# ELU in the last layer: the clamp to negative values leaves VectorE, and the final step becomes a maximum against the pre-activation

## The chip, the cores and the metric

The kernel runs on one core of one Trainium2 chip. The metric is the device time of one execution in microseconds. PE is TensorE (PEld its weight loads), ACT is ScalarE, DVE is VectorE, POOL is GpSimd, and SP issues most of the DMAs.

## The reference

Three layers follow one another: attention with pooled queries, a mixture of eight experts of which each token uses two, and a dense layer with an ELU. Only the last one is touched. Its input `x` has 1152 rows of 512 values, `w_in` is 512 x 2048 and `w_out` is 2048 x 512:

```python
def _moe2_ref(x, w_in, w_out):
    h = x @ w_in
    alpha = 1.0
    g = np.where(h > 0.0, h, alpha * (np.exp(np.minimum(h, 0.0)) - 1.0))
    return (g @ w_out).astype(np.float32)
```

## The kernel before, in words

The whole program is scheduled by hand: each helper files its steps on a time line (`Line.at(t, step)`), the steps are sorted by that time, and the sorted order is the program order on every engine. Each engine then works through its own queue in that order and waits on semaphores. The planned times set only the order.

Every matrix product is done in split precision. A float32 value is held as a high part (rounded, made by a copy on ACT) and a low part (value less high part, made by a subtraction on DVE or POOL), and three matmul passes, high x high, low x high and high x low, add up in PSUM.

The last layer works in three chunks of 384 rows (`ch` 0 to 2). In a chunk, the 2048 hidden columns are 16 steps `f` of 128 columns. Three functions in `plan_moe2` (line 959 on) belong to each step:

- `l1(f)`: 12 matmuls into a PSUM tile `a` of 128 x 384 (line 972). There are three such tiles, each in a bank of its own.
- `act(f)`: the ELU from `a` to `r`, and the split of `r` into `g2h` (ACT, line 981) and `g2l` (DVE, line 982). The tiles `r` and `m` have two buffers each, `g2h` and `g2l` three.
- `outs(f)`: nine matmuls into three PSUM tiles `o` that run over all 16 steps (line 991). Of each three the first two read `g2h`, and the third reads `g2l`.

On PE the order is l1(0), l1(1), l1(2), outs(0), l1(3), outs(1), and so on, since `outs(f)` is filed two steps behind `l1(f)`.

While chunk 0 runs, the second halves of `w_in` and `w_out` are still brought in, in eight pieces of 128 x 1024 (`plan_weight`, line 681). For each piece SP loads `raw` (line 668, six buffers), ACT copies it into the high part `wh` (line 670), and POOL subtracts to get the low part `wl` (line 674). On ACT these copies stand between the ELU steps, in the order act(0), piece 0, act(1), pieces 1 and 2, act(2), piece 3, act(3), piece 4, act(4), pieces 5 and 6, act(5), piece 7, act(6). From act(7) on ACT has no weight pieces. For chunks 1 and 2 the expert outputs are gathered by POOL (line 942), mixed on DVE (lines 947 and 948), transposed on PE (line 955) and split (lines 956 and 957), while the chunk before is still at work.

In the experts, line 733 is an operation on DVE with the same kinds of operands as the changed last step of the ELU: one input in PSUM, one in SBUF, the result in SBUF.

Of the kernel before, what the change touches and what calls it, by code (L numbers as in the profile page):

```python
# [5 lines left out]
AF=mybir.ActivationFunctionType; OP=mybir.AluOpType; AX=mybir.AxisListType  # L6
# [135 lines left out]
def ap(src, off, dims):  # L142
    return bass.AP(tensor=src.tensor, offset=src.offset+off, ap=dims)
# [819 lines left out]
def plan_moe2(ln, tc, ch, t0, xs_, win, wout, out, gp, xp, ps):  # L963
    nc=tc.nc; O={}; G={}
    def l1(f):
        xh,xl=xs_['x']
        a=G['a',f]=ps.tile([128,512],FT,tag="a",name="a2",bufs=3)
        wh,wl=win[f//8]['w']; fs=slice((f%8)*128,(f%8)*128+128)
        n=0
        for wv,xv in ((wh,xh),(wl,xh),(wh,xl)):  # L970
            for c in range(4):
                nc.tensor.matmul(a[:,0:384],wv[:,c,fs],xv[:,c],start=n==0,stop=n==11); n+=1  # L972
    def act(f):
        a=G.pop(('a',f))
        r=gp.tile([128,384],FT,name="r2"); m=gp.tile([128,384],FT,name="m2")
        nc.scalar.activation(r,a[:,0:384],AF.Relu)  # L976
        nc.vector.tensor_scalar(m,a[:,0:384],0.0,None,op0=OP.min)  # L977
        nc.scalar.activation(m,m,AF.Exp)  # L978
        nc.vector.scalar_tensor_tensor(r,m,-1.0,r,op0=OP.add,op1=OP.add)  # L979
        gh=gp.tile([128,384],FR,name="g2h",bufs=3); gl=gp.tile([128,384],FR,name="g2l",bufs=3)  # L980
        nc.scalar.activation(gh,r,AF.Copy)  # L981
        nc.vector.tensor_tensor(gl,r,gh.bitcast(FT),op=OP.subtract)
        G[f]=(gh,gl)
    def outs(f):
        if f==0:
            for i in range(3): O[i]=ps.tile([128,512],FT,tag="o",name="o2",bufs=3)
        wh,wl=wout[f//8]['w']; gh,gl=G.pop(f)
        for i in range(3):
            ts=slice(i*128,i*128+128)
            for n,(gv,wv) in enumerate(((gh,wh),(gh,wl),(gl,wh))):  # L990
                nc.tensor.matmul(O[i],gv[:,ts],wv[:,f%8],start=f==0 and n==0,stop=f==15 and n==2)  # L991
    def fin(i):
        tt=3*ch+i
        y=xp.tile([128,512],FT,name="yg0",bufs=3) if ch==2 else gp.tile([128,512],FT,name="out_sb",bufs=2)
        if i%2: nc.vector.tensor_copy(y,O[i])
        else: nc.scalar.activation(y,O[i],AF.Copy)
        if tt<8:
            b,j=divmod(tt,4)
            nc.sync.dma_start(ap(out,(b*576+j)*512,[[2048,128],[1,512]]),y)
        else:  # L1000
            for b,e in enumerate((nc.sync,nc.scalar)):
                e.dma_start(ap(out,(b*576+512)*512,[[512,64],[1,512]]),y[64*b:64*b+64])
    d=3.87
    for f in range(16):
        ln.at(t0+d*f+(.05 if f==0 else 0),l1,f); ln.at(t0+d*f+1.0,act,f); ln.at(t0+d*(f+2)+.1,outs,f)
    for i in range(3): ln.at(t0+d*17+.2+.01*i,fin,i)
# [132 lines left out]
```

## Time and profile before

| what | value |
|---|---|
| median of 3 runs | 825.7 us (825.38 to 841.67) |
| the profiled execution | 819.85 us |
| its span, first to last instruction | 818.1 us |
| PE busy | 786.0 us, 96% of the span |
| DVE busy | 585.6 us, 72% |
| ACT busy | 482.4 us, 59% |
| POOL busy | 328.2 us, 40% |

The span leaves out 1.75 us of the profiled execution, ahead of its first and behind its last instruction. The last layer's matmuls begin 606.3 us into the span. Busy shares are averages over the whole span; what a change in the last layer is worth is read from the stretch from there on.

### The profile page before, as it was taken

Reading aid. Unit: us, or ns where it says so; the run is one execution under the profiler, and the core shown is the slowest. Engines: PE = TensorE matmul, PEld = TensorE weight load, DVE = VectorE, ACT = ScalarE, POOL = GpSimd, SP = SyncE. Lnnn points to the kernel's source line nnn. Section 1 sums busy time; section 2 is a strip of 40 time slices with the busy share of each in tenths; the row PEclk is TensorE's granted clock in tenths of the full one; section 3 lists DMA queues with packets and bytes.
Section 4 is the critical chain, followed back from the end, with each engine's and each line's share of the span. In section 5 each row is a group of like instructions: output and inputs, shape, how many; then the busy total and the mean of one; then the engine's idle time right before and its main releaser. Section 6 shows DMA issues by size and latency. Waiting matters only on the chain.

```text
span 818.1 us, 13530 instructions
## 1 busy us (share of the span) xinstructions
PE 786.0 (96%) x4891; PEld 721.4 (88%) x4891; DVE 585.6 (72%) x1182; ACT 482.4 (59%) x1109; POOL 328.2 (40%) x303
## 2 busy tenths in 40 slices
PE   7999999999999999989999999999999899999997
PEld 5898989998888889979899999999887799999996
DVE  6888898898999876586968778687555644454443
ACT  5988888989888864434444445445345434334432
POOL 4634051431510765266666677666516602000000
PEclk8999999999999999989999999999999999999999
DMA  8029465131002245559688898986743203001001
GB/s 251 2 93 274 136 230 178 40 128 57 29 30 105 91 138 198 187 179 309 228 287 262 274 306 279 295 275 218 263 125 115 64 14 104 1 14 38 1 1 40
DMA packets 50984, 119.82 MB, mean 146 GB/s; under 512 B 7574, under 2 KB 8598, under 8 KB 50914
## 3 DMA queue, kind: packets, MB, share of 16 engines
q1 hardware_dynamic: 47922, 109.35, 40.6%
q0 software_dynamic: 2912, 9.44, 3.6%
q8 instruction: 40, 0.66, 0.3%
q14 instruction: 30, 0.25, 0.1%
q10 hardware_dynamic: 80, 0.13, 0.0%
HBM read 82.89 MB, written 36.01 MB: 145 GB/s over the span
## 4 chain that ended last, share of the span: by engine, by line
PE 30%; DMA 11%; DVE 9%; ACT 3%; issue 2%; POOL 2%; SPq 0%; DVEq 0%; POOLq 0%; ACTq 0%
PE o L991 11%; PE a L972 10%; PE oe L741 5%; DMA raw<-in_moe_w_in_dram 5%; DMA raw<-in_moe_w_dram 3%; PE ae L731 3%; DVE wl L674 2%; DMA raw<-in_moe_w_out_dram 2%; ACT wh L670 1%; DVE cvt L703 1%; DVE cvm L701 1%; DVE r L979 1%; DMA raw<-wf 1%; POOL cvm L708 1%; DVE cvt L704 1%
## 5 line engine op out<-in xcount | busy, mean ns | idle before, releaser
L293 ACT ACTIVATE p<-sp,m 128x384 f32<-128x384 f32 x216 | 125.1, 585 | 13.2 <-DVE m L285 13.0
L282 DVE TENSOR_REDUCE m<-sp 128x1 f32<-128x384 f32 x216 | 115.4, 550 | 20.6 <-PE sp L277 18.8
L674 POOL TENSOR_TENSOR wl<-raw,wh 128x1024 fp32r<-128x1024 f32 x32 | 80.8, 2530 | 59.3 <-ACT wh L670 59.2
L670 ACT ACTIVATE wh<-raw 128x1024 fp32r<-128x1024 f32 x76 | 79.8, 1057 | 37.9 <-DMA raw<-in_moe_w_dram 36.7
L305 DVE TENSOR_TENSOR pl<-t_p,ph 128x512 fp32r<-128x512 f32 x144 | 96.8, 683 | 6.0 <-ACT ph L302 4.2
L302 ACT ACTIVATE ph<-t_p 128x512 fp32r<-128x512 f32 x144 | 86.2, 603 | 16.7 <-PE t_p L299 11.3
L299 PE MATMUL t_p<-ident,p 128*128 128x128 f32 x576 | 83.3, 274 | 1.2 <-ACT xt L363 0.7
L277 PE MATMUL sp<-khl,qh 128*128 128x384 f32 x192 | 75.6, 394 | 4.2 <-ACT p L293 3.7
L299 PEld LDWEIGHTS t_p<-ident,p 128*128 128x128 f32 x576 | 67.9, 140 | 9.9 <-ACT xt L363 0.9
L707 POOL TENSOR_SCALAR cvm<-cvm 128x512 f32<-128x512 f32 x32 | 51.3, 1602 | 38.9 <-DVE cvm L701 38.9
L277 PE MATMUL sp<-khl,ql 128*128 128x384 f32 x192 | 65.7, 342 | 0.0
L674 DVE TENSOR_TENSOR wl<-raw,wh 128x1024 fp32r<-128x1024 f32 x44 | 63.4, 1453 | 2.6 <-ACT wh L670 2.6
L310 PE MATMUL o<-ph,vhl 128*128 128x512 f32 x144 | 63.8, 443 | 0.0
L991 PE MATMUL o<-wh,g2h 128*128 128x512 f32 x144 | 57.1, 396 | 3.9 <-ACT g2h L981 3.9
L234 POOL TENSOR_SCALAR kr<-kraw 128x576 fp32r<-128x576 f32 x14 | 9.5, 678 | 126.2 <-PE t_k L241 126.2
L311 PE MATMUL o<-pl,vhl 128*128 128x512 f32 x144 | 57.3, 398 | 1.0 <-DVE pl L305 1.0
L991 PE MATMUL o<-wh,g2l 128*128 128x512 f32 x144 | 56.8, 394 | 0.0
L991 PE MATMUL o<-wl,g2h 128*128 128x512 f32 x144 | 56.3, 391 | 0.0
L977 DVE TENSOR_SCALAR m<-a 128x384 f32<-128x384 f32 x48 | 26.7, 556 | 40.9 <-ACT r L976 40.2
L708 POOL TENSOR_TENSOR cvm<-cvm,cvt 128x512 f32<-128x512 f32 x32 | 48.0, 1501 | 17.3 <-DVE cvt L704 17.3
L979 DVE SCALAR_TENSOR_TENSOR r<-m,r 128x384 f32<-128x384 f32 x48 | 34.3, 714 | 28.4 <-ACT m L978 27.8
L701 DVE TENSOR_SCALAR cvm<-raw 128x512 int32<-128x512 int32 x32 | 26.9, 839 | 34.8 <-DMA raw<-in_moe_w_in_dram 19.9
(269 smaller groups left out, 1987.4 us busy)
## 6 DMA issues: line engine op xcount, KB each, us to landing
raw<-in_moe_w_dram SPq DMA_DIRECT2D x60, 512.0 KB, 7.1
raw<-in_moe_w_in_dram SPq DMA_DIRECT2D x16, 512.0 KB, 7.7
wf<-cvm SPq DMA_DIRECT2D x32, 256.0 KB, 2.8
raw<-in_moe_w_out_dram SPq DMA_DIRECT2D x16, 512.0 KB, 8.3
raw<-wf SPq DMA_DIRECT2D x16, 512.0 KB, 4.6
xs<-zrow SPq DMA_DIRECT2D x3, 1792.0 KB, 15.1
xs<-zrow SPq DMA_DIRECT2D x2, 2560.0 KB, 22.9
xe<-xs SPq DMA_DIRECT2D x7, 672.0 KB, 9.4
```

Of the source, the lines that this page charges most:

```text
L277: nc.tensor.matmul(sp[:,g,0:384],w,kh[:,h,384*(g0+g):384*(g0+g)+384],start=i==0,stop=i==len(ops)-1)
L282: nc.vector.tensor_reduce(m[:,x:x+1],s['s',j,x][:,:,0:384],axis=AX.XY,op=OP.max,negate=True)
L293: nc.scalar.activation(s['p',j][:,384*g0:384*(g0+nb)].rearrange("p (g n) -> p g n",g=nb),s.pop(('s',j,x))[:,:,0:384],AF.Exp,bias=m[:,3:4], ...
L299: nc.tensor.transpose(t[:,jj*128:jj*128+128],s['p',4*h+jj][:,kt*128:kt*128+128],ident)
L302: nc.scalar.activation(ph,s['tp',h,kt],AF.Copy)
L305: nc.vector.tensor_tensor(pl,s.pop(('tp',h,kt)),s['ph',h,kt].bitcast(FT),op=OP.subtract)
L310: nc.tensor.matmul(s['o',h],w,s.pop(('ph',h,kt)),start=kt==0,stop=False)
L311: nc.tensor.matmul(s['o',h],w,s.pop(('pl',h,kt)),start=False,stop=kt==8)
L670: s.tc.nc.scalar.activation(w[0][:,p['i']*p['n']:(p['i']+1)*p['n']],p['r'],AF.Copy)
L674: e.tensor_tensor(w[1][:,sl],p['r'],w[0][:,sl].bitcast(FT),op=OP.subtract)
L972: nc.tensor.matmul(a[:,0:384],wv[:,c,fs],xv[:,c],start=n==0,stop=n==11); n+=1
L991: nc.tensor.matmul(O[i],gv[:,ts],wv[:,f%8],start=f==0 and n==0,stop=f==15 and n==2)
```

## The change

The ELU took four instructions per step: Relu on ACT, a minimum with zero on DVE, Exp on ACT, and on DVE the sum of (exp less one) and the Relu. It now takes three: ACT computes Relu(-h), then Exp of the negative of that, and DVE takes the maximum of (exp less one) and h, which it reads from PSUM. The split that follows is as it was.

```diff
     def act(f):
         a=G.pop(('a',f))
         r=gp.tile([128,384],FT,name="r2"); m=gp.tile([128,384],FT,name="m2")
-        nc.scalar.activation(r,a[:,0:384],AF.Relu)
-        nc.vector.tensor_scalar(m,a[:,0:384],0.0,None,op0=OP.min)
-        nc.scalar.activation(m,m,AF.Exp)
-        nc.vector.scalar_tensor_tensor(r,m,-1.0,r,op0=OP.add,op1=OP.add)
+        nc.scalar.activation(m,a[:,0:384],AF.Relu,scale=-1.0)
+        nc.scalar.activation(m,m,AF.Exp,scale=-1.0)
+        nc.vector.scalar_tensor_tensor(r,m,-1.0,a[:,0:384],op0=OP.add,op1=OP.max)
         gh=gp.tile([128,384],FR,name="g2h",bufs=3); gl=gp.tile([128,384],FR,name="g2l",bufs=3)
         nc.scalar.activation(gh,r,AF.Copy)
         nc.vector.tensor_tensor(gl,r,gh.bitcast(FT),op=OP.subtract)
```

## Rows read from the trace of the kernel before

**Rows 1.** Chain that ended last, from the page: shares of the span by engine

```profile
PE 30%; DMA 11%; DVE 9%; ACT 3%; issue 2%; POOL 2%; SPq 0%; DVEq 0%; POOLq 0%; ACTq 0%
```

**Rows 2.** Stretches of the last layer: length, busy us (x instructions) per engine, PEclk, DMA

```profile
606.30:645.50 39.20, 35.27 (x174) 30.07 (x173) 21.56 (x26) 19.56 (x34) 21.80 (x11) 1.00 0.37 119
...
672.00:690.00 18.00, 18.00 (x99) 16.41 (x98) 7.26 (x14) 7.46 (x16) 4.92 (x5) 1.00 0.38 117
690.00:740.00 50.00, 50.00 (x257) 45.56 (x256) 25.19 (x46) 19.55 (x39) 0.94 (x1) 1.00 0.02 6
```

**Rows 3.** Timeline, PE, starts of l1(3), l1(10) and l1(12) in chunk 0

```profile
614.96 0.86 PE L972 MATMUL a<-x2h,wh 128*128 128x384 f32 x4
...
649.48 0.86 PE L972 MATMUL a<-x2h,wh 128*128 128x384 f32 x4
...
657.75 0.86 PE L972 MATMUL a<-x2h,wh 128*128 128x384 f32 x4
```

**Rows 4.** Single lines: the ELU's instructions, duration ns min/median/max, first and last start

```profile
L976 ACT ACTIVATE r<-a x48: 469/493/499, 609.1 to 807.5; 128x384 f32<-128x384 f32 x48
L977 DVE TENSOR_SCALAR m<-a x48: 548/558/559, 609.6 to 808.0; 128x384 f32<-128x384 f32 x48
L978 ACT ACTIVATE m<-m x48: 523/525/528, 610.2 to 808.6; 128x384 f32<-128x384 f32 x48
L979 DVE SCALAR_TENSOR_TENSOR r<-m,r x48: 557/558/2728, 610.7 to 809.2; 128x384 f32<-128x384 f32 x48
L981 ACT ACTIVATE g2h<-r x48: 522/525/527, 611.3 to 809.8; 128x384 fp32r<-128x384 f32 x48
L982 DVE TENSOR_TENSOR g2l<-r,g2h x48: 557/559/561, 611.9 to 810.3; 128x384 fp32r<-128x384 f32 x48
```

**Rows 5.** Timeline, pieces 1 and 2, act(2) and outs(2): start us, us, [idle before <-releaser]

```profile
616.16 1.99 ACT L670 ACTIVATE wh<-raw 128x1024 fp32r<-128x1024 f32 x2
...
617.29 4.74 POOL L674 TENSOR_TENSOR wl<-raw,wh 128x1024 fp32r<-128x1024 f32 x2 [2.00 <-ACT wh L670]
...
618.06 0.47 ACT L976 ACTIVATE r<-a 128x384 f32<-128x384 f32 x1
...
618.57 0.56 DVE L977 TENSOR_SCALAR m<-a 128x384 f32<-128x384 f32 x1 [1.72 <-ACT r L976]
...
619.16 0.53 ACT L978 ACTIVATE m<-m 128x384 f32<-128x384 f32 x1 [0.62 <-DVE m L977]
619.72 2.73 DVE L979 SCALAR_TENSOR_TENSOR r<-m,r 128x384 f32<-128x384 f32 x1 [0.59 <-ACT m L978]
...
622.48 0.52 ACT L981 ACTIVATE g2h<-r 128x384 fp32r<-128x384 f32 x1 [2.79 <-DVE r L979]
...
623.03 0.56 DVE L982 TENSOR_TENSOR g2l<-r,g2h 128x384 fp32r<-128x384 f32 x1 [0.59 <-ACT g2h L981]
623.05 0.50 PE L991 MATMUL o<-wh,g2h 128*128 128x512 f32 x1 [1.72 <-ACT g2h L981]
```

**Rows 6.** Waits in the last layer, 606 us on: us in total, times, longest

```profile
PEld o L991 <- ACT g2h L981: 5.1, 5, 2.5
PE o L991 <- ACT g2h L981: 3.9, 2, 2.2
```

**Rows 7.** Timeline in the experts: DVE beside a POOL subtraction

```profile
473.17 2.89 POOL L674 TENSOR_TENSOR wl<-raw,wh 128x1024 fp32r<-128x1024 f32 x1 [0.46 <-ACT wh L670]
474.37 0.51 DVE L733 SCALAR_TENSOR_TENSOR hl<-ae,hh 128x336 fp32r<-128x336 f32 x1 [0.57 <-ACT hh L732]
474.79 1.55 DVE L701 TENSOR_SCALAR cvm<-raw 128x512 int32<-128x512 int32 x1
```

**Rows 8.** Single lines: DVE with an input in PSUM, weight subtractions, duration ns min/median/max

```profile
L733 DVE SCALAR_TENSOR_TENSOR hl<-ae,hh x56: 493/501/510, 363.8 to 581.5; 128x336 fp32r<-128x336 f32 x56
...
L957 DVE TENSOR_TENSOR x2l<-t,x2h x8: 548/553/560, 673.3 to 744.0; 128x384 fp32r<-128x384 f32 x8
...
L674 POOL TENSOR_TENSOR wl<-raw,wh x32: 2365/2407/3340, 337.7 to 639.6; 128x1024 fp32r<-128x1024 f32 x32
```

**Rows 9.** Timeline, DVE: an instruction that reads what the one before it wrote

```profile
651.82 0.48 DVE L947 TENSOR_SCALAR yg<-yg,wt 128x512 f32<-128x512 f32 x1
652.33 0.75 DVE L948 SCALAR_TENSOR_TENSOR yg<-yg,wt,yg 128x512 f32<-128x512 f32 x1
```

**Rows 10.** Groups of ACT instructions: a function table load (mean ns)

```profile
L448 ACT ACT_TABLE_LOAD x2 | 2.6, 1283 | 0.0
```

**Rows 11.** Timeline, SP: loads of the eight pieces, with the time their issue took

```profile
604.16 15.91 SPq L668 DMA_DIRECT2D raw<-wf x8
```

## The prediction

> **What bounds the kernel now.** The chain of waits comes first: half of its attributed time is PE, and DVE and ACT together have 12% [rows 1]. That is the whole program; the change touches only the last layer, so the stretches of that layer come next. [...] The first stretch, 606.3 to 645.5, is different: PE is busy 35.27 of 39.20 us. So the gain must come from there, if from anywhere.
>
> How much is lost there is read best from the spacing of l1. Seven steps lie between l1(3) and l1(10): 649.48 - 614.96 = 34.52 us, where seven undisturbed ones take 7 x 4.135 = 28.94 us [rows 3]. PE loses 5.58 us. The waits say to whom: TensorE's matmuls and weight loads of outs wait for g2h [rows 6]. (The 3.9 us of idle PE are two long gaps; the other 1.7 us are matmuls stretched because their weights come late.)
>
> Why g2h is late is seen at act(2) [rows 5]. Two things add up. First, the ELU is a relay between two engines, with ACT held in its queue meanwhile: Relu at 618.06, the minimum at 618.57, although it reads nothing that the Relu writes (both read the same PSUM bank, and the second reader starts when the first has ended), Exp at 619.16. Second, the last DVE step, line 979, takes 2.73 us, where its median is 0.558 [rows 4, 5]. It starts 0.06 us after the second of POOL's two subtractions must have begun (617.29 + half of 4.74 = 619.66), and ends 0.42 us after POOL's end at 622.03. Both of its inputs lie in SBUF, as POOL's do. Over 48 instructions only six are long, at the six steps in which a piece of weights is being subtracted; line 982, also with two SBUF inputs, always comes after the stall and never exceeds 0.561 us [rows 4]. Meanwhile ACT waits 2.79 us for DVE, and the next weight copy and Relu are queued behind that wait on ACT.
>
> **The change part by part.** *The minimum goes.* 48 x 0.558 = 26.8 us of DVE time are removed [rows 4]. On the path of a step Relu start to Exp start was 619.16 - 618.06 = 1.10 us [rows 5]; it becomes the Relu, 0.49 us, and a handover from ACT to itself. The trace before has no ACT instruction that reads what the one before it on ACT wrote. The nearest row is DVE's pair, where the reader starts 0.03 us after the writer's end (651.82 + 0.48 = 652.30 to 652.33) [rows 9]; the far one is a table load of 1.28 us in between [rows 10]. I take 0.03, since both are in-order engines that hand over a tile; the lower bound is an overlapped start, some 0.1 us less. The path is shorter by 1.10 - 0.52 = 0.58 us per step.
>
> *The scale of -1* is an operand of ACT instructions that exist already. Nothing is added; I keep 0.493 and 0.525 us [rows 4].
>
> *The last DVE step reads PSUM in place of one SBUF tile.* Its undisturbed price: line 957, one input in PSUM and 384 columns, has 0.553 us, where line 982 with two SBUF inputs has 0.559 [rows 4, 8]. I take 0.558, so nothing. [...]
>
> Its disturbed price is the larger point. The same kind of instruction, line 733, starts at 474.37 in the middle of a POOL subtraction (473.17 to 476.06) and takes 0.51 us; none of its 56 exceeds 0.510, while the neighbour of 474.79, of another kind, stretches to 1.55 us, 0.28 us past POOL's end [rows 7, 8]. So I expect line 979's successor to pass POOL, and the excess of the six stalls, 0.77 to 2.17 us each (1.33 to 2.73 less 0.56), to leave the path from Relu to g2h.
>
> *The stall goes to g2l.* It still has two SBUF inputs and now arrives while POOL works. I let it end 0.42 us after POOL, as line 979 did [rows 5]. Behind it on DVE stands only the next step's maximum, and on PE the third of each three matmuls.
>
> *The tile `a` is held until the maximum ends*, 0.16 + 0.49 + 0.03 + 0.53 + 0.03 + 0.56 = 1.8 us after l1, and l1(f+3) comes three steps later, over 10 us. No cost.
>
> **The sum, step by step.** I lay out chunk 0 with these durations: Relu 0.49, Exp 0.53, maximum 0.56, g2h 0.53, handovers 0.03, a weight copy 1.05 (0.1 of it overlapped), POOL 2.41 [rows 4, 5, 8]. ACT's round of a step is 2.2 us plus its pieces. With PE undisturbed, outs(f) starts at 612.90 + 4.135 f (614.96 less the 2.06 of outs(0)). Then:
>
> - act(1): Relu 612.1, g2h done 614.3, g2l 615.1 (POOL's piece 0 ends 614.7). Needed 617.0.
> - act(2): pieces 1 and 2 copied 614.2 to 616.2, POOL on them 615.3 to 620.1; Relu 616.1, g2h 618.3, g2l 620.1 + 0.42 = 620.5. Needed 621.2. Before: g2h 623.0.
> - act(3): Relu 619.2, g2h 621.6, g2l 622.9. Needed 625.3.
> - act(5): pieces 5 and 6 copied 624.6 to 626.6, POOL until 630.5; g2h 628.7, g2l 630.9. Needed 633.6. Before: 638.6.
>
> All are in time, with at least 0.6 us to spare. All of the 5.58 us is regained. The weights don't stand in the way: six of the eight loads were issued ahead of the ELU, the last two wait for a `raw` buffer [rows 11], which piece 0 frees at 614.7 instead of 615.3. Later stretches stay as they are, since PE has no idle time to give back [rows 2], and everything shifts with it.
>
> Span: 818.1 - 5.6 = 812.5 us; profiled execution 819.85 - 5.6 = 814.3. The median of the runs before lies 5.9 us above the profiled execution. I put the same 5.6 us on it: **825.7 - 5.6 = 820.1 us**, 0.7% less.
>
> **The rivals.** *(A) The stalls stay half on the path.* Either the maximum still waits for POOL, or POOL's subtractions, delayed by DVE, take the 3.34 us that the longest had [rows 8]. With the first, act(2)'s g2l ends at 621.9 and act(5)'s at 635.5, so that outs(2) loses 0.4 and outs(5) 1.2 us: 1.6 of the 5.6 us remain, 821.7 us. With the second, POOL ends pieces 1 and 2 at 622.0 and g2l ends 622.4, some 0.8 us too late, and again at pieces 5 and 6: also 821.7. [...] The six stalls before show VectorE as the loser each time.
>
> *(B) Nothing is gained.* PE finds another late input: the weight pieces, or at the chunk borders the gathered rows. For: ACT and POOL are both busier in the first stretch than later. Against: act(7) on has no pieces, and between 672 and 690, at a chunk border, PE has no gap [rows 2]. 825.7 us.
>
> *(C) It is slower: Exp behind its own Relu waits on ACT.* If the handover costs x more than 0.03 us, every step's round on ACT grows by x. In the seven steps with weight pieces the margin is used up at x = 0.5 us; at 1.3, a table load's length, 3.1 us are lost and the gain is 2.5 (823.2); from about x = 1.65 on the kernel is slower than before. From 2.0 on the round, 2.2 + x, exceeds PE's 4.135 in all 48 steps, and near x = 2.3 the kernel is some 2% slower. Against: Relu, Exp and Copy already alternate on ACT and no table load stands in the last layer; all of ACT's waits there have other names.
>
> **How the numbers follow.** Forecast 0.77, (A) 0.10, (B) 0.08, (C) with a time above 825.7 0.05. The likeliest is 820.1. The range: downward the whole gain on the level of the profiled execution, 814.3; upward it takes in (A) and (B) with the runs' spread of 0.3 us, 826. Faster or slower by over 2% (about what a measurement of this kernel can tell from no change) means 16.5 us, three times what PE loses here: faster 0.01, slower 0.03, within 0.96.
>
> **What would show it.** Right: seven steps from l1(3) to l1(10) in 28.9 us; no PE wait for g2h; the maximum at 0.55 to 0.57 us in all 48; line 982's longest growing from 0.56 to about 2.2 us; Exp starting 0.5 us after Relu. Wrong: a maximum over 1 us (A); PE waiting for g2l (A) or a weight (B); a gap between Relu and Exp (C). The sum is wrong as a whole if the median and the profiled execution do not move together.

## The result, and the profile after

| | before | changed |
|---|---|---|
| median of 7 runs each | 825.7 us (815.79 to 841.67) | 809.97 us (808.61 to 822.57) |
| ratio | | 0.9849, 95% interval 0.9809 to 0.9889 |
| profiled execution, its span | 819.85 us, 818.1 us | 822.57 us, 820.8 us |
| mean granted clock in the profiled execution | 0.990 | 0.980 |

By the ratio the changed kernel is 1.5% faster, some 12.5 us; the medians of the table lie 15.7 us apart. The prediction said 5.6 us, and 809.97 lies below its range. The executions of either kernel differ in how long TensorE was granted only half its clock (0.50) ahead of the last layer: every ratio in this document leaves out the longest ones, which the medians and ranges include, and as the profiled execution of the changed kernel is one of these, the traces are compared by stretches of the last layer and not by their spans.

The same stretch as in [rows 2], counted from the first l1 of each kernel (length, then busy us and instructions of PE, PEld, DVE, ACT, POOL, then PEclk, DMA share and GB/s):

```profile
614.60:653.80 39.20, 39.15 (x203) 35.95 (x202) 19.49 (x25) 23.19 (x40) 25.05 (x13) 1.00 0.45 146
698.00:748.00 50.00, 50.00 (x259) 45.36 (x258) 18.15 (x33) 18.86 (x38) 0.95 (x1) 1.00 0.02 6
```

PE is busy in 39.15 of 39.20 us, where it had 35.27, and handles 203 matmuls instead of 174. Later stretches were full and are full (50.00 of 50.00 us in both). The starts of l1(3) and l1(10), as in [rows 3]:

```profile
623.31 0.86 PE L972 MATMUL a<-x2h,wh 128*128 128x384 f32 x4
...
652.24 0.86 PE L972 MATMUL a<-x2h,wh 128*128 128x384 f32 x4
```

That is 28.93 us for the seven steps, 5.59 less than the 34.52 of [rows 3]. It is 4.133 us a step, where an undisturbed one took (657.75 - 649.48) / 2 = 4.135 [rows 3]: no time is left between them. From the first l1 to the last outs the layer takes 201.6 us against 207.2. The single lines of the ELU, as in [rows 4] (duration ns min/median/max):

```profile
L976 ACT ACTIVATE m<-a x48: 469/492/502, 617.4 to 810.2; 128x384 f32<-128x384 f32 x48
L977 ACT ACTIVATE m<-m x48: 523/523/527, 617.9 to 810.7; 128x384 f32<-128x384 f32 x48
L978 DVE SCALAR_TENSOR_TENSOR r<-m,a x48: 541/555/555, 618.5 to 811.3; 128x384 f32<-128x384 f32 x48
L981 DVE TENSOR_TENSOR g2l<-r,g2h x48: 557/559/2358, 619.7 to 812.4; 128x384 fp32r<-128x384 f32 x48
```

The last step, now line 978, never exceeds 0.555 us; the longest was 2.728. The subtraction, now line 981, has taken the stalls over: 2.358 where the longest was 0.561. Act(2) in the timeline, as in [rows 5]:

```profile
623.67 17.87 POOL L674 TENSOR_TENSOR wl<-raw,wh 128x1024 fp32r<-128x1024 f32 x7 [0.62 <-ACT wh L670]
624.45 0.47 ACT L976 ACTIVATE m<-a 128x384 f32<-128x384 f32 x1
624.95 0.53 ACT L977 ACTIVATE m<-m 128x384 f32<-128x384 f32 x1
625.51 0.55 DVE L978 SCALAR_TENSOR_TENSOR r<-m,a 128x384 f32<-128x384 f32 x1 [2.04 <-ACT m L977]
626.10 0.53 ACT L980 ACTIVATE g2h<-r 128x384 fp32r<-128x384 f32 x1 [0.62 <-DVE r L978]
...
626.66 2.20 DVE L981 TENSOR_TENSOR g2l<-r,g2h 128x384 fp32r<-128x384 f32 x1 [0.59 <-ACT g2h L980]
```

Relu to Exp is 0.50 us instead of 1.10; the maximum runs while POOL subtracts and is not held; g2h follows at once; g2l is held and nothing on PE waits for it. Of the waits of PE on ACT and DVE in the ELU [rows 6] none is left. So the last layer did what the forecast says: 5.59 us where 5.58 were forecast. The rest, some 7 us by the ratio and 10 by the medians, is the question.

### The profile page after: what moved, and what is told of

Read it like the earlier page. It is cut to its first block, busy times and chain, and to the rows that moved or that the text cites. A ratio compares the mean times of both kernels' runs of the same rounds, so it can differ in the third digit from the quotient of the medians.

```text
span 820.8 us, 13443 instructions
## 1 busy us (share of the span) xinstructions
PE 790.5 (96%) x4891; PEld 728.2 (89%) x4891; DVE 559.7 (68%) x1134; ACT 483.1 (59%) x1109; POOL 328.1 (40%) x303
## 4 chain that ended last, share of the span: by engine, by line
PE 31%; DMA 11%; DVE 10%; issue 2%; POOL 2%; ACT 1%; SPq 0%; DVEq 0%; POOLq 0%; ACTq 0%
PE a L972 12%; PE o L990 12%; DMA raw<-in_moe_w_in_dram 4%; DMA raw<-in_moe_w_out_dram 4%; PE oe L741 3%; DVE wl L674 3%; PE ae L731 3%; DVE cvt L703 2%; DVE cvm L701 2%; DVE cvt L704 1%; DMA ys<-ye 1%; POOL cvm L708 1%; DVE hl L733 1%; PE ac L922 1%; DVE cvt L702 1%
## 5 line engine op out<-in xcount | busy, mean ns | idle before, releaser
L978 DVE SCALAR_TENSOR_TENSOR r<-m,a 128x384 f32<-128x384 f32 x48 | 26.6, 554 | 86.3 <-ACT m L977 86.2
L976 ACT ACTIVATE m<-a 128x384 f32<-128x384 f32 x48 | 23.4, 488 | 64.4 <-PE a L972 64.4
L981 DVE TENSOR_TENSOR g2l<-r,g2h 128x384 fp32r<-128x384 f32 x48 | 33.4, 695 | 28.4 <-ACT g2h L980 28.4
```

## The experiments

### Is the rest of the gain the change, or the clock?

First the changed kernel and the kernel before were run again, unaltered, in the same session.

> The changed kernel once more, timed beside the kernel before. Two theories for why the whole gained 12.5 us at the medians when the last layer should give 5.6. Theory 1 (the rest is the granted clock of the runs drawn, not the change): each run's time goes with its mean granted clock, about 8.2 us per 0.01 of clock missing; carried to a clock of 1.00 the changed kernel is at 806 us and the kernel before at 811.7, 5.6 apart, and the ratio of the medians moves towards 0.993 as runs are added. Theory 2 (the change itself gives some 6 us more, somewhere ahead of the last layer or in it): at equal clock the two stay 10 to 12 us apart, or the changed kernel's runs have the higher clock time after time and the ratio stays at 0.985. Either way the trace's last layer, from its first l1 matmul to its last outs matmul, takes 201.2 us against 207.2 before.

> The kernel before against itself. Theory 1: the ratio is 1.00, but its runs scatter over 10 us or more with the granted clock (0.98 to 0.995), so a comparison of medians can be off by several us. Theory 2: its runs lie within 3 us of one another and the ratio is 1.000 with a narrow interval.

| | runs | median | mean clock of the runs | ratio to before |
|---|---|---|---|---|
| before | 35 | 818.79 us | 0.959 to 0.998 | |
| the same, again | 12 | 823.89 us | 0.961 to 0.994 | 1.005, 1.0014 to 1.0086 |
| changed | 12 | 814.84 us | 0.960 to 0.997 | 0.9951, 0.9909 to 0.9993 |

The ratio of the changed kernel moved from 0.985 to 0.995. Six of the first seven runs of the changed kernel had a mean clock of 0.991 to 0.997; of these twelve only half had 0.99 or more. The kernel before differs from itself by 5 us at the median and by half a per cent in the ratio, with an interval that leaves out 1; that is nearly as much as the effect looked for (5.6 us, 0.7%). The time follows the clock closely. Over all 94 runs of the kernel before that list their clock and the 31 of the changed one, both with the later ones below, a straight line with one slope for both gives 7.5 us per 0.01 of clock (8.2 were expected), and at equal clock the changed kernel is 5.1 us faster (standard error 0.4). With the runs of 0.975 and more alone it is 5.4 us. Theory 1 holds: at equal clock 5 to 5.5 us, the rest was which runs were drawn. The layer itself takes 201.6 us in this trace too; the 201.2 in the expectation was 0.4 too low.

Where the clock is lost stands in the traces. This is the end of attention, first in the changed kernel's first trace, then in its second:

```profile
300.00:310.00 10.00, 9.04 (x62) 8.31 (x61) 6.80 (x34) 5.64 (x12) 0.68 (x3) 0.86 0.89 311
310.00:320.00 10.00, 10.00 (x57) 9.98 (x57) 4.34 (x25) 3.43 (x4) 1.23 (x2) 0.50 0.02 8
320.00:330.00 10.00, 10.00 (x49) 8.44 (x48) 2.82 (x6) 1.41 (x4) 8.43 (x15) 0.79 0.54 176
```

```profile
300.00:310.00 10.00, 9.03 (x76) 8.44 (x75) 6.88 (x40) 5.03 (x10) 0.68 (x3) 1.00 0.82 305
310.00:320.00 10.00, 10.00 (x78) 8.84 (x76) 6.02 (x20) 4.12 (x7) 6.28 (x9) 1.00 0.30 86
```

In the first PE runs at a granted clock of 0.50 for some 17 us, and does 57 matmuls from 310 to 320 us, for which the second, at 1.00, shows 78. What PE did before it is the same in both, with two short gaps. First the trace in which the clock fell, behind the second gap, then the one in which it stayed:

```profile
305.53 0.29 PE L367 MATMUL t_l<-wd,xt 128*64 128x16 f32 x2 [0.31 <-ACT xt L363]
306.43 0.34 PE L844 MATMUL a<-x0h,w0h 128*128 128x168 f32 x1 [0.61 <-DVE L L371]
```

```profile
304.09 0.29 PE L367 MATMUL t_l<-wd,xt 128*64 128x16 f32 x2 [0.31 <-ACT xt L363]
304.99 0.34 PE L844 MATMUL a<-x0h,w0h 128*128 128x168 f32 x1 [0.61 <-DVE L L371]
```

Both have 0.31 and 0.61 us of idle time in front of the same instructions. So have all eleven traces here of kernels whose gaps are as they were (0.60 in two), and the clock falls there in six of them, for some 17 us or more, and not in the other five. The first trace of the kernel before, on which the prediction rests, is one of the five. What decides whether it falls is not shown.

### Which part of the change gives the 5.6 us?

Two things were changed in the last layer: the relay ACT, DVE, ACT, DVE lost one hand-over, and the last step lost one of its two SBUF inputs. Three kernels take them apart. The first changes the last step alone (against the kernel before):

```diff
         nc.scalar.activation(r,a[:,0:384],AF.Relu)
         nc.vector.tensor_scalar(m,a[:,0:384],0.0,None,op0=OP.min)
         nc.scalar.activation(m,m,AF.Exp)
-        nc.vector.scalar_tensor_tensor(r,m,-1.0,r,op0=OP.add,op1=OP.add)
+        nc.vector.scalar_tensor_tensor(r,m,-1.0,a[:,0:384],op0=OP.add,op1=OP.max)
```

> Only the last line of the ELU is changed: the maximum of (exp less one) and the pre-activation in PSUM. The Relu on ScalarE and the minimum on VectorE stay, the Relu's result being overwritten unread. Theory 'port' (what cost PE its 5.6 us is the last VectorE step waiting for POOL, since both its inputs lay in SBUF): the last step is 0.55 us in all 48, the subtraction g2l takes the stalls, PE waits for nothing, the last layer takes 201.2 to 201.7 us like the changed kernel's. Theory 'relay' (the hand-overs ACT, DVE, ACT cost it): the Relu to Exp time stays 1.1 us and most of the loss stays, the last layer takes 204 us or more.

The second shortens the relay but keeps both inputs in SBUF (against the changed kernel):

```diff
         nc.scalar.activation(m,a[:,0:384],AF.Relu,scale=-1.0)
         nc.scalar.activation(m,m,AF.Exp,scale=-1.0)
-        nc.vector.scalar_tensor_tensor(r,m,-1.0,a[:,0:384],op0=OP.add,op1=OP.max)
+        nc.scalar.activation(r,a[:,0:384],AF.Relu)
+        nc.vector.scalar_tensor_tensor(r,m,-1.0,r,op0=OP.add,op1=OP.add)
```

> The other part alone: the minimum on VectorE goes, ScalarE makes Relu(-h), Exp and Relu(h), and the last VectorE step adds (exp less one) and the Relu, both in SBUF as before. Theory 'port': the last step is stretched again in six steps, and PE loses 1.2 to 5.5 us, how much depending on whether the step starts just before or just after POOL's second subtraction; the last layer takes 202.5 to 207 us. Theory 'relay': the loss goes, 201.2 to 201.7 us.

The third keeps the clamp on VectorE and drops the Relu (against the kernel before):

```diff
-        nc.scalar.activation(r,a[:,0:384],AF.Relu)
         nc.vector.tensor_scalar(m,a[:,0:384],0.0,None,op0=OP.min)
         nc.scalar.activation(m,m,AF.Exp)
-        nc.vector.scalar_tensor_tensor(r,m,-1.0,r,op0=OP.add,op1=OP.add)
+        nc.vector.scalar_tensor_tensor(r,m,-1.0,a[:,0:384],op0=OP.add,op1=OP.max)
```

> The ELU in three steps the other way: the clamp stays on VectorE as a minimum, the Relu on ScalarE goes, Exp, and the maximum against PSUM. Theory 'port': the operand is what counts, so 28.9 to 29.3 us from l1(3) to l1(10) and the same time as the changed kernel within 0.5 us at equal clock, although VectorE keeps its 26.7 us of minima. Theory 'relay' (it is the step moved off VectorE that counts): 31 us or more.

The last step of the three, in that order (duration ns min/median/max):

```profile
L979 DVE SCALAR_TENSOR_TENSOR r<-m,a x48: 553/555/556, 616.1 to 809.3; 128x384 f32<-128x384 f32 x48
```

```profile
L979 DVE SCALAR_TENSOR_TENSOR r<-m,r x48: 557/559/2479, 607.4 to 803.1; 128x384 f32<-128x384 f32 x48
```

```profile
L978 DVE SCALAR_TENSOR_TENSOR r<-m,a x48: 553/555/556, 618.9 to 812.1; 128x384 f32<-128x384 f32 x48
```

The starts of l1(3) and l1(10), in the same order:

```profile
620.34 0.86 PE L972 MATMUL a<-x2h,wh 128*128 128x384 f32 x4
...
649.59 0.86 PE L972 MATMUL a<-x2h,wh 128*128 128x384 f32 x4
```

```profile
611.88 0.86 PE L972 MATMUL a<-x2h,wh 128*128 128x384 f32 x4
...
643.73 0.86 PE L972 MATMUL a<-x2h,wh 128*128 128x384 f32 x4
```

```profile
623.64 0.86 PE L972 MATMUL a<-x2h,wh 128*128 128x384 f32 x4
...
652.57 0.86 PE L972 MATMUL a<-x2h,wh 128*128 128x384 f32 x4
```

| kernel | l1(3) to l1(10) | of the 5.59 us | median of the runs, clock of its trace |
|---|---|---|---|
| before | 34.52 us | 0 | |
| operand alone | 29.25 us | 5.27 | 819.90 us (12 runs), 0.981 |
| relay alone | 31.85 us | 2.67 | 823.58 us (12 runs), 0.996 |
| clamp on VectorE | 28.93 us | 5.59 | 818.09 us (4 runs), 0.980 |
| changed | 28.93 us | 5.59 | |

The medians of these runs do not order them, since their clocks spread as those of the table above (ratios to before 0.9954, 0.9905 to 1.0003, for the operand; 0.9984, 0.9929 to 1.0039, for the relay; 0.9841, 0.976 to 0.9923, for the clamp, from four runs); the stretch does. Theory 'port' holds ('port' is a name only: the runs show the wait for POOL, not what in the chip causes it): with the PSUM operand alone, and the whole relay kept, all but 0.3 us are gained. These 0.3 us put the layer at 201.96 us, just above the 201.2 to 201.7 expected: a weight load waits once, 0.5 us, for g2l. With the relay shortened and the operands in SBUF, half remains lost, inside the 202.5 to 207 us expected (the layer takes 204.5 us). What PE waits for there is no longer g2h but g2l (us in total, times, longest):

```profile
PE o L991 <- DVE g2l L982: 2.2, 2, 1.4
```

The last step reaches VectorE just ahead of POOL's second subtraction in act(2) and act(5) and takes 0.61 us, and g2l, right behind it, is held for 2.08 and 2.06 us. And the clamp may stay on VectorE at no cost in this stretch; over the whole layer that kernel takes 201.94 us against 201.59, with one wait of 0.5 us for an output copy on ACT at a chunk's end. So shortening the relay, for which the minimum goes, gives about half by itself and nearly nothing on top of the PSUM operand. The two parts do not add up, since either one takes the last step of act(2) and act(5) out of the wait for POOL's second subtraction; what gives nearly all is where the last step reads.

### Does VectorE lose to POOL by order of arrival?

In [rows 5] the last step came 0.06 us after POOL's second subtraction and waited for all of it. If order of arrival decides, added POOL work between the two should help. First one memset of one element, then four, ahead of each subtraction but the very first (two lines that pass in the tile and mark the seven subtractions with 'm' are left out):

```diff
+        if eng=='m':
+            for _ in range(4): s.tc.nc.gpsimd.memset(s.sp,0.0)
         e=s.tc.nc.vector if eng=='v' else s.tc.nc.gpsimd
         e.tensor_tensor(w[1][:,sl],p['r'],w[0][:,sl].bitcast(FT),op=OP.subtract)
```

> The kernel before, with work added: a memset of one element (0.09 us) on POOL ahead of each of the weight subtractions of the last layer but the very first. Theory 'port': in the kernel before the last ELU step came to VectorE 0.06 us after POOL had begun the second of two subtractions, and so waited for the whole of it; with the memset it comes while POOL is in the first, is served between the two, and the two stalls of 2.7 us shrink to some 0.6 to 1.0 us. The seven steps l1(3) to l1(10) then take 29.5 to 31 us in place of 34.5 and the whole gets 3.5 to 5 us faster at equal clock, although nothing was taken away. Theory 'relay' (the hand-overs, not the port): 34.5 us as before or a little more.

> The kernel before with four one-element memsets on POOL in place of one ahead of each weight subtraction. One moved the second subtraction of a pair only from 2.37 to 2.40 us behind the first, and the ELU step still came 0.03 us too late at 2.43. Four should move it to 2.6 or more. Theory 'port' with service in order of arrival: the ELU step now arrives while nothing or only the first subtraction holds the port, the two stalls of 2.7 us shrink to 1.0 or less, and l1(3) to l1(10) takes 29.5 to 31.5 us in place of 34.5, or of 35.8 where the clock falls. If the order of arrival does not decide: 34 us or more.

Timeline of act(2) with one memset, then with four:

```profile
619.81 0.09 POOL L673 MEMSET spacer<- 1x1 f32 x1
619.87 2.38 POOL L675 TENSOR_TENSOR wl<-raw,wh 128x1024 fp32r<-128x1024 f32 x1
619.90 2.76 DVE L980 SCALAR_TENSOR_TENSOR r<-m,r 128x384 f32<-128x384 f32 x1 [0.59 <-ACT m L979]
```

```profile
624.55 0.53 POOL L674 MEMSET spacer<- 1x1 f32 x4
624.65 0.56 DVE L981 SCALAR_TENSOR_TENSOR r<-m,r 128x384 f32<-128x384 f32 x1 [0.59 <-ACT m L980]
625.09 2.39 POOL L676 TENSOR_TENSOR wl<-raw,wh 128x1024 fp32r<-128x1024 f32 x1
...
625.80 2.09 DVE L984 TENSOR_TENSOR g2l<-r,g2h 128x384 fp32r<-128x384 f32 x1 [0.59 <-ACT g2h L983]
```

One memset was too little: the step still arrives 0.03 us late and takes 2.76 us, and the seven steps take 35.63 us. That number alone is what theory 'relay' expected, and the 29.5 to 31 us of theory 'port' were missed; only the timeline shows why. With four, of which there is a single run, it arrives ahead of the second subtraction and takes 0.56 us, there and in act(5), without any change to the ELU: when it arrives decides. The gain is less than expected, 32.59 us against 29.5 to 31.5, because g2l is then held for 2.09 us and PE waits for that:

```profile
PE o L993 <- DVE g2l L984: 2.6, 2, 1.4
```

That is the effect of rival (A) of the prediction, a late g2l, in a kernel where g2h comes late enough for g2l to matter. The whole times, 825.47 us (median of 4 runs) and 823.19 (one run), are too few to compare.

Taking POOL out of the stretch is the other way to the same end:

```diff
-MW=((0,2,3),(12,14,3),'pppp','pppp')
+MW=((0,2,3),(12,14,3),'vvvv','vvvv')
```

> The kernel before with the eight weight subtractions of the last layer moved from POOL to VectorE (1.2 us each in place of 2.4), so that POOL holds nothing while the ELU runs. Theory 'port': all 48 last steps take 0.56 us; VectorE has 9.8 us more to do in its queue, so that some of PE's loss stays: l1(3) to l1(10) takes 30 to 32 us. Theory 'relay': 34 us or more, since the relay is unchanged and VectorE is busier.

All 48 last steps take 0.557 to 0.561 us, and the seven steps 31.40 us (from 635.79 to 667.19), as theory 'port' has it: no stalls, but VectorE's own weight work in their place.

```profile
L979 DVE SCALAR_TENSOR_TENSOR r<-m,r x48: 557/559/561, 631.6 to 826.9; 128x384 f32<-128x384 f32 x48
```

The median is 821.47 us (11 runs; the ratio to before is 0.9945, 0.989 to 0.9999).

### Can the clock be held?

If the drop at the end of attention follows the two short gaps, filling them should end it. The result of the added matmuls is not used:

```diff
+            if u==7:
+                for _ in range(3): nc.tensor.matmul(t[:,128:256],ident,ident,start=True,stop=True)
             nc.tensor.matmul(t[0:64,0:16],s['xt'],wd[:,hp],start=True,stop=True)
+            if u==7:
+                z=ps.tile([128,512],FT,tag="t",name="t_z",bufs=TB)
+                for _ in range(4): nc.tensor.matmul(z[:,0:128],ident,ident,start=True,stop=True)
```

> The changed kernel with seven matmuls of the identity added where attention ends, in two gaps of TensorE (0.3 and 0.6 us) after which its clock fell to half in three of six traces and not in the other three. They leave the result as it is. If the drop follows those two gaps: no run with the drop at 305 to 325 us, so the runs with a mean clock of 0.978 to 0.985 go and the median falls to 809 to 812 us. If it does not hang on gaps this short: the clocks are spread as before, about half of the runs at 0.985 or below, median 812 to 818 us.

> The changed kernel with the seven added identity matmuls, once more, beside the next two kernels on one chip. Before, all six runs of it had a mean clock of 0.993 or more. Theory 1 (the added matmuls keep the clock up where attention ends): again no run below 0.988, median 808 to 813 us, while the same chip gives the kernels without them runs at 0.96 and 0.98. Theory 2 (a lucky draw): half of its runs at 0.985 or below, median 812 to 818.

The kernel before, with the same lines, and the changed kernel without them ran beside the second:

> The kernel before with the same seven added matmuls, so that the ELU is compared without the draw of the clock. Theory 1 (the first comparison's 12.5 us were 5.6 of ELU and the rest clock): its runs lie at 0.988 or more too, its median at 813 to 818 us, 5 to 6 above the changed kernel with the same matmuls, and one to two more where TensorE's wait of 2.2 us in the last layer lets the clock fall once more. Theory 2: 10 us or more apart at equal clock.

> The changed kernel unaltered, beside the two. Theory 1: its clocks are spread again (some 0.96, some 0.98, some 0.995), its median 812 to 818 us, its fastest runs 808 to 811 as with the added matmuls. Theory 2 (the change itself holds the clock): all but one at 0.99 or more, as in its first seven runs.

| one chip, same session | runs | median | range | mean clock of the runs | ratio to before |
|---|---|---|---|---|---|
| before | 30 | 824.72 us | 814.37 to 843.71 | 0.956 to 0.996 | |
| changed | 12 | 818.43 us | 809.27 to 836.16 | 0.963 to 0.997 | 0.9929, 0.9879 to 0.9979 |
| before, gaps filled | 12 | 820.07 us | 815.62 to 823.99 | 0.988 to 0.996 | 0.9989, 0.9953 to 1.0025 |
| changed, gaps filled | 12 | 813.01 us | 808.91 to 815.25 | 0.991 to 0.996 | 0.9912, 0.9878 to 0.9946 |

The first six runs of the filled changed kernel, on another chip, have a median of 811.02 us and clocks of 0.993 to 0.998 (ratio 0.9835, 0.9787 to 0.9882). With these, all 30 runs of either kernel with the gaps filled have 0.988 or more, where 13 of the changed kernel's 31 runs without have less, and 48 of the 94 of the kernel before. Three medians of this table lie above what was expected, by 0.01 us for the filled changed kernel, by 2.1 us for the filled kernel before and by 0.4 us for the changed one; the clocks are as theory 1 has them. The end of attention in a trace of the filled changed kernel, where each added matmul shows as two instructions:

```profile
304.68 0.29 PE L369 MATMUL t_l<-wd,xt 128*64 128x16 f32 x2
304.90 1.16 PE L372 MATMUL t_z<-ident 128*128 128x128 f32 x8
306.11 0.35 PE L849 MATMUL a<-x0h,w0h 128*128 128x168 f32 x1
```

PE has no gap over 0.05 us there, and PEclk stays 1.00 in this trace from 300 us until 350 us. In none of the three traces of filled kernels does the clock fall at the end of attention. So it is shown that the added matmuls end the drop; whether what counts is the idle time that they fill or the work that they add is not shown. The seven matmuls have a price: from the transpose ahead of the first gap (line 359) to line 844, here 849, it takes 2.50 us in this trace and 1.49 in the second trace of the changed kernel. Over many runs the changed kernel with the gaps filled is ahead of both kernels: 813.01 us on this chip against 818.43 and 824.72, and its longest run is shorter than the median of either. It gains by having no long runs: its shortest run, 808.91 us, is hardly better than the 809.27 without, and the ratios, 0.9912 and 0.9929, are not told apart.

With that disturbance out of the way, the ELU's worth can be read from whole runs: 820.07 - 813.01 = 7.1 us. With 12 runs each, which scatter by some 2 us, a 95% interval is about 5 to 9 us, so the medians alone do not tell 7.1 from 5.6. The trace of the filled kernel before shows where more than 5.6 comes from. This is PE's wait at outs(5) of chunk 0, and two stretches of 2 us around it, in the columns of the stretches above:

```profile
641.52 0.50 PE L996 MATMUL o<-wh,g2h 128*128 128x512 f32 x1 [2.18 <-ACT g2h L986]
```

```profile
640.00:642.00 2.00, 0.48 (x2) 0.30 (x2) 1.41 (x2) 1.05 (x2) 0.50 (x1) 1.00 0.00 0
642.00:644.00 2.00, 2.00 (x7) 1.50 (x6) 0.64 (x3) 1.31 (x3) 1.50 (x1) 0.53 0.00 0
```

Behind PE's wait of 2.2 us for g2h at outs(5), the granted clock falls, to a mean of 0.53 over the second of these stretches, and PE does 7 matmuls in its 2 us. The seven steps take 35.84 us instead of 34.52 (from 617.82 to 653.66), and the layer 208.49 us, 6.9 more than in the changed kernel. The trace of the repeated kernel before has the same (35.78 and 208.49 us), and that with one memset too (35.63 us); the first trace of before, on which the prediction rests, is the one of four where the clock held. In none of the ten traces without that wait does the layer show such a fall: outside of the seven steps it takes 172.65 to 173.01 us in them, against 172.68 in the first trace of before, and the changed kernel's first trace has a granted clock of 1.00 in every stretch from 600 to 807 us.

## Why the prediction was right or wrong

**The mechanism in the last layer was right at each step.** The gain sits where it was put, between l1(3) and l1(10): 5.59 us measured, 5.58 forecast. Counted from l1(3), act(2)'s g2h was done at 618.28 (forecast 618.3) and its g2l at 620.51 (620.5), act(5)'s at 628.53 and 630.93 (628.7, 630.9). The hand-over from Relu to Exp on ACT, bounded only by far rows, cost 0.03 us (624.45 + 0.47 to 624.95), so rival (C) had no place. The PSUM input had no price of its own: undisturbed, the last step took 0.555 us with it and 0.558 without (medians). What it changed is the wait for POOL: the last step took 0.556 us at most in the kernel with the operand alone and 2.728 in the kernel before, which differ in this step only.

**One price inside was off, without effect:** POOL's subtractions, 2.41 us each in the layout, took 17.87 / 7 = 2.55 in a row. In the timeline four of the seven start while a held g2l is finishing, and take 2.55 to 2.73 us; the other three take 2.40 or 2.41. (A) named that direction.

**What failed is the step from the sum to the time:** "The median of the runs before lies 5.9 us above the profiled execution. I put the same 5.6 us on it." It takes the 5.9 us between the median of three runs and the profiled execution for a property of the kernel. In the changed kernel the median lies 12.6 us below its profiled execution (809.97 and 822.57), so this term of the sum came out with the other sign. The prediction had named the sign of it: the median and the profiled execution did not move together, one fell by 15.7 us and the other rose by 2.7. The range rested on the same term, with a spread of the runs of 0.3 us, although one of the three runs ahead of the prediction took 841.67 us.

It was a draw: the kernel before has runs from 813 to 844 us, and its medians in four sessions are 825.7, 818.8, 824.1 and 824.7. Six of the first seven runs of the changed kernel had a mean clock of 0.991 or more; of its other 24 runs half have less than 0.988, and if half fall, at most one of seven does in one case of sixteen (an estimate). The seven of the kernel before do not list their clock; their median is that of its runs at 0.975 to 0.9875 (825.9 us, 33 of 94). The change does not touch the end of attention, so the part of the 1.5% beyond the ELU was luck of the draw, as far as the later runs show; whether the first comparison's chip also held the clock better is open. On the level of runs at a clock of 0.9915 to 0.9945, which 9 of the 31 of the changed kernel have, its median is 811.7 and that of before 817.1 (30 of 94): 5.4 us apart.

The page of the profile had a hint: in its row of PEclk one slice in the middle stands at 8, and windows of 25 us show 0.86 and 0.93 between 350 and 400 us. These are other drops than that at the end of attention, which this trace does not have, but they show that the clock falls ahead of the last layer; the prediction looked at it only inside. A range for the time of a kernel with such drops had to reach down to the profiled execution's own clock made good, by estimate 819.85 less 7.5 for its missing 0.01, less 5.6: 807 us. The shortest run was 808.61.

**A second, smaller term was missing:** a wait of 2.2 us of PE can cost more than itself. In three of four traces with that wait the clock fell behind it, 1.1 to 1.3 us more. The forecast counted the stretch from the one trace without it. The change's own worth is 5.6 us where the clock holds and about 7 where it falls.

Rival (B) fell: PE found no other late input. Rival (A) did not happen in the changed kernel; a late g2l did cost PE time in the kernel with the relay alone and in the one with four memsets.

## What to carry to other kernels

When an instruction on VectorE is long only at times, look at what POOL runs then: here, reading one of its inputs where the matmul left it, in PSUM, took it past POOL, and that was worth more (5.27 us) than removing a whole instruction from the engine (2.67 us). Before a change of under 1% is costed or compared, list the mean granted clock of the runs; compare at equal clock, or first fill the gaps on TensorE behind which it falls.

## What the runs showed of the hardware that was not expected

- The same program with the same two gaps of 0.31 and 0.61 us on TensorE has its clock halved behind them in some executions and not in others: in six of eleven traces, for some 17 us in five of these and some 58 in the sixth, a run at a mean clock of 0.965. With seven small matmuls in those gaps none of three traces has the drop, and none of 30 runs a mean clock below 0.988.
- Each of the six held last steps in the trace of before ended 0.41 or 0.42 us after a POOL subtraction (in act(2), 622.03 to 622.45). In the changed kernel g2l of act(2) came at 626.66, during the second of seven subtractions in a row (626.04 to 628.44), and ended at 628.86, 0.42 us behind it; it did not wait for the third, which began at 628.41 and took 2.73 us. With one memset in the kernel before, the last step of act(2) came 0.03 us after the second subtraction had begun, and took 2.76 us in place of 0.56.
- A one-element memset on POOL takes 0.09 us, but moved the instruction behind it by only 0.03 us (2.37 to 2.40 us behind the first subtraction), as it began 0.07 us before the subtraction ahead of it ended (619.81, and 617.47 + 2.41 = 619.88).
